# A written-out order of engine work: planner costs, a fourth output buffer, and a later values' product

## The chip, the cores and the metric

The kernel runs on one core of a Trainium2 chip. The metric is the device time of one execution in microseconds (us). Engines in the rows: PE is TensorE's matmul, PEld its weight load, DVE is VectorE, ACT is ScalarE, POOL is GpSimd, and SP is SyncE, which in this kernel issues nearly all transfers (SPq in the rows is its queue).

## The reference, cut to what matters

Three layers follow each other: windowed attention (B = 4 batches, 8 heads, S = 576 tokens, width 64), a gated layer with a spatial product over the tokens, and, last, four experts that are themselves causal attentions. The change touches only the experts' layer:

```python
logits = x @ w_gate                      # top 2 of E = 4 experts, softmax over them -> w
for e in range(E):
    q, k, v = x @ wq[e], x @ wk[e], x @ wv[e]
    scores = scale * (q @ k.transpose(0, 2, 1))
    scores = np.where(causal, -1e9, scores)
    a = softmax(scores)                  # over all 576 keys, causal
    ye = a @ v @ wo[e]
    out += (w of expert e, 0 if not chosen) * ye
```

The layer before it hands over one 512-wide row for each token; the product with its output weights is folded into wq, wk and wv.

## The kernel before, in words

All matmuls are 32-bit: a factor is split into a high part (a rounded copy, on ACT) and a low part (source minus high part, a subtraction), and three passes of products are added up (PASSES). PE's order is the order in which the Python code calls the matmuls. For the first two layers the order of the other engines is a list of names or is left to the compiler's scheduler. For the experts' layer a planner, class Flow, writes the order of ACT, DVE, POOL and SP while the PE code is generated: it keeps a clock `pe` of what PE has been given, and chains of items `(engine, ns, operation, after, ok)`. An item is put into its engine's order when, by the planned costs, the item before it in its chain is done (its `ns`, then `after`) and the engine is free. On the chip each engine runs its own order strictly, and semaphores hold an instruction until its operands and buffers are there; a planned cost is never a wait on the chip, it only sets places in the orders.

The experts' layer goes through 20 tiles, one for each batch b and block j of rows (j = 0 to 3 are 128 rows with 128, 256, 384 and 512 keys, j = 4 is the last 64 rows with all 576). For step s of the loop:

- `scores_b(*tiles[s])` (matmuls of L1084, and L1088 for j = 4) writes scores into two PSUM buffers (psS). Then, by the planner: row minima on DVE (L1114 or L1119), exponentials on ACT (L1115, L1124), the sums' inverses times the gates on DVE (L1136 to L1138), the scaling of the rows on POOL (`scale_rows`, L309), a transpose within blocks of 32 on DVE (L1162), four sends on SP to DRAM (`mid<-pB`, L1164), and one read back on SP (`read_back`, `pTB<-mid`, L1181; two for j = 4). The trip over DRAM completes the transposition. The buffers of the weights before (p) and after the trip (pT) are three each.
- `close_tile(tiles[s - LAG])`, LAG = 4, is the values' product of the tile four steps back: 16 to 40 matmuls L1234 that read pTB, then its copy `o` on ACT (L1247) and low part on DVE; and the tile's output product joins the list of work `todo`.
- five calls of `pull` take pieces from `todo`: the projections of the next batch (`proj`, `pq` L1022 and `pvB` L992) and the output products (`out_tile`, `pout`, six matmuls L1276), each followed by a copy to `ot` on ACT (L1281) and a store on SP (L1283, L1285). `ot` has 3 buffers, `o` has 11 (OBUFS) for each part.

In the last steps three tiles (y, a, z in the code: rows 2, 1, 0 of the last batch) are transposed on PE instead (`turn_b`, `ptB`, L1206, copied by L1212); `turn_b(y)` stands in step 18, the last of the loop, and the scores of z behind it.

`load_g(b)` brings the input of batch b in four chunks of 288 KB (`gf<-g_dram`, L887): for each chunk a high part on ACT (`x<-gf`, L894), a low part on POOL (`lo_part`, L274), and at the end the same for a tail (`both`, L903). Batch 0's is written before the planner starts, batch 1's is its first chain, and those of batches 2 and 3 run beside the steps.

Of the kernel before, what the change touches and what calls it, by code (L numbers as in the profile page):

```python
# [10 lines left out]
F32 = mybir.dt.float32  # L11
# [11 lines left out]
B, H, S, D = 4, 8, 576, 64  # L23
P = 128
DM = 512
# [7 lines left out]
FLT_MAX = 3.0e38  # L33
TOK = [(t * 128, min(128, S - t * 128)) for t in range(5)]
COL = [64, 192, 320, 448, 0]
OBUFS = 11
PASSES = ((0, 0), (0, 1), (1, 0))
ORDER = ((0, 1, 2, 3, 4), (4, 0, 1, 2, 3))
OPENING = """
# [202 lines left out]
def item(engine, ns, op, after=0.0, ok=None):  # L242
    return engine, ns, op, after, ok
# [3 lines left out]
def block_kernel(ctx, tc, qP, kP, v, w_in, wspT, bsp, w_outT, wcat, wo, relt, tri, out):  # L247
    nc = tc.nc
# [24 lines left out]
    def lo_part(lo, src, hi, engine=nc.vector):  # L273
        engine.tensor_sub(lo, src, hi.bitcast(F32))  # L274
# [56 lines left out]
    back, over, first, both = (t[:, :P] for t in u)  # L331
# [548 lines left out]
    both = []  # L880

    def load_g(b, pool):
        G = x if b % 2 == 0 else x2
        f = pool.tile([P, 4, S], F32, tag="gf", name=f"gf{b}", bufs=1)

        def fetch(k, after=0.0):
            return "SP", 400.0, lambda: nc.sync.dma_start(f[:, k, :], g_dram[b, k]), after, None  # L887

        def parts():
            first = 2 if b > 1 else 4  # L890
            for k in range(first):
                yield fetch(k, 6000.0 if k == first - 1 else 0.0)
            for k in range(4):
                yield "ACT", 626.0, lambda k=k: nc.scalar.copy(G[0][:, k, :S], f[:, k, :]), 0.0, None  # L894
                yield "POOL", 900.0, lambda k=k: lo_part(G[1][:, k, :S], f[:, k, :], G[0][:, k, :S], nc.gpsimd), 3000.0 if b > 1 and 0 < k < 3 else 0.0, None
                if k + first < 4:
                    yield fetch(k + first)
            c = slice(64 * (b % 2), 64 * (b % 2) + 64)

            def high():  # L900
                if b % 2 == 0:
                    both[:] = [gfp.tile([P, 4, P], F32R, tag=f"both{i}", name=f"both{b}_{i}") for i in range(2)]
                nc.scalar.copy(both[0][:, :, c], f[:, :, 0:64])  # L903

            yield "ACT", 400.0, high, 0.0, lambda: tails_done[0] >= b // 2
            yield "POOL", 500.0, lambda: lo_part(both[1][:, :, c], f[:, :, 0:64], both[0][:, :, c], nc.gpsimd), 0.0, None

        return G, list(parts())

# [11 lines left out]
    wk = ctx.enter_context(tc.tile_pool(name="wk", bufs=2, reuse_waits="tile"))  # L921
    wos = [wk.tile([P, 2, DM], F32R, name=f"wo{i}", bufs=1) for i in range(2)]
    for k in range(2):
        st = wk.tile([P, DM], F32, tag="ot", name=f"st_wo{k}", bufs=3)
        nc.sync.dma_start(st, wo[k * P : (k + 1) * P, :])
        split(wos[0][:, k, :], wos[1][:, k, :], st)
    x2 = [wk.tile([P, 4, S], F32R, name=f"x2{i}", bufs=1) for i in range(2)]
# [5 lines left out]
    flow = Flow()  # L933
# [8 lines left out]
    def leave(n, *items, delay=250.0):  # L942
        banks[n] = flow.add(items, rank=0, delay=delay)
        return banks[n]
# [206 lines left out]
    def cross_items(b, j):  # L1151

        p = sb_[b, j][0]
        e = 4 if j < 4 else 2
        n, w = (4 * (j + 1), 128) if j < 4 else (18, 64)
        mid = dram.tile([16 if j < 4 else 18, 32, 4, w], F32, tag=f"mid{w}", name=f"mid{b}_{j}", bufs=3)
        me = state[b, j]
        items = []
        cuts = [0, n * w] if n < 12 else [0, n * w // 2, n * w]
        for c0, c1 in zip(cuts, cuts[1:]):  # L1160
            flat = p[:, c0:c1]
            items.append(item("DVE", 130.0 + 1.12 * (c1 - c0), lambda flat=flat: nc.vector.transpose(flat, flat)))  # L1162
        def send(q):
            nc.sync.dma_start(mid[:n, :, q, :].rearrange("k i w -> i k w"), p[32 * q : 32 * q + 32, : n * w].rearrange("i (k w) -> i k w", w=w))  # L1164
            me["written"] = q == 3

        items += [item("SP", 500.0, lambda q=q: send(q), 0.0 if q < 3 else 5000.0) for q in range(4)]
        items.append(item("SP", 400.0, lambda: read_back(b, j, mid), 5000.0, lambda: tiles.index((b, j)) < 3 or tiles[tiles.index((b, j)) - 3] in closed))
        items.append(item("PE", 0.0, lambda: me.update(read=True)))
        return items  # L1170

# [2 lines left out]
    def read_back(b, j, mid):  # L1174
        e = 4 if j < 4 else 2
        n, w = (4 * (j + 1), 128) if j < 4 else (18, 64)
        cs = (n + 3) // 4
        pT = wk.tile([P, 16 * P], F32, tag="pT", name=f"pTB{b}_{j}", bufs=3)
        for c0, m, rows in ((0, n // 4, 128),) if j < 4 else ((0, 4, 128), (4, 1, 64)):
            src = mid[4 * c0 : 4 * c0 + rows // 32 * m].rearrange("(c k) i a w -> (k i) c (a w)", c=m)  # L1180
            nc.sync.dma_start(pT[:rows, c0 * 4 * w : (c0 + m) * 4 * w].rearrange("i (c w) -> i c w", c=m), src)  # L1181
        full = pT[:, : cs * 4 * w].rearrange("p (c a e q) -> p c a e q", a=4, e=e, q=32)

        def rhs(pr, c, o):
            kb = 64 if c == 4 else 128
            return full[:, c, :, 2 * pr + o, :] if j < 4 else full[:kb, c, 2 * o : 2 * o + 2, pr, :]

        sb_[b, j] = rhs
# [60 lines left out]
        flow.work(400.0 + (2 * (j + 1) * 212.0 if j < 4 else 2 * 9 * 120.0))  # L1249

    taken = {}
    stored = deque()

    def out_tile(b, t):
        flow.finish(taken[b, t])
        t0, tn = TOK[t][0], P
        o2 = OT.pop((b, t))
        if (b, t) == tiles[-1]:
            ot = wk.tile([P, DM], F32, tag="ot", name=f"ot{b}_{t}", bufs=3)
            for h, copy in enumerate((nc.vector.tensor_copy, nc.scalar.copy)):  # L1260
                c = slice(256 * h, 256 * h + 256)
                at, po = bank(f"pout{b}_{t}_{h}")
                n = 0
                for i, j in PASSES:
                    for pr in range(2):
                        nc.tensor.matmul(po[:, :256], o2[i][:, pr, :], wos[j][:, pr, c], start=(n == 0), stop=(n == 5))
                        n += 1
                leave(at, item(("DVE", "ACT")[h], 400.0, lambda copy=copy, c=c, po=po: copy(ot[:, c], po[:, :256])),
                      item(("SP", "ACT")[h], 400.0, lambda h=h, c=c: (nc.sync, nc.scalar)[h].dma_start(out[b, t0 : t0 + tn, c], ot[:, c])))
                yield 6 * 120.0  # L1270
            return
        at, po = bank(f"pout{b}_{t}")
        n = 0
        for i, j in PASSES:
            for pr in range(2):
                nc.tensor.matmul(po[:tn], o2[i][:, pr, :tn], wos[j][:, pr, :], start=(n == 0), stop=(n == 5))  # L1276
                n += 1
            if n < 6:
                yield 2 * 231.0
        ot = wk.tile([P, DM], F32, tag="ot", name=f"ot{b}_{t}", bufs=3)  # L1280
        items = [item("ACT", 580.0, lambda: nc.scalar.copy(ot[:tn], po[:tn]))]  # L1281
        if t < 4:
            items.append(item("SP", 400.0, lambda: nc.sync.dma_start(out[b, t0 : t0 + tn, :], ot)))  # L1283
        else:
            items += [item("SP", 500.0, lambda i=i: nc.sync.dma_start(out[b - 1 + i, t0:S, :], ot[64 * i : 64 * i + 64])) for i in range(2)]  # L1285
        stored.append(leave(at, *items))
        if len(stored) > 2:
            flow.finish(stored.popleft())
        yield 2 * 231.0


# [31 lines left out]
    def close_tile(t):  # L1323
        at, px = attend_b(*t)
        take_b(*t, at, px)
        b1, j1 = t
        if j1 < 4 or b1 % 2:
            todo.append(out_tile(b1, j1))
# [5 lines left out]
    for s in range(len(tiles) - 1):  # L1334
        b, j = tiles[s]
        if s % 5 == 0:
            if p_next is not None:
                through(p_next)
            if b + 1 < B:
                flow.finish(ahead)  # L1340
                p_next = proj(b + 1, G)
                todo.appendleft(p_next)
            if b + 2 < B:
                G, ahead = load(b + 2)
        if s >= 1:
            ready(tiles[s - 1])
        if s >= 3:
            flow.until(lambda: state[tiles[s - 3]]["written"])
        scores_b(*tiles[s])
        if s >= LAG:  # L1350
            close_tile(tiles[s - LAG])
        for i in range(5):
            pull((5500.0 if s < 1 else RATE if s < 15 else 4600.0 if s < 18 else 2000.0) / 5)
            if tiles[s] == a and i == 1:
                turn_b(*y)
            if tiles[s] == a and i == 3:
                ready(a)
                for chain in state[y]["home"]:
                    flow.finish(chain)
                flow.until(lambda: state[tiles[s - 2]]["written"])  # L1360
                scores_b(*z)
# [83 lines left out]
```

## Time and profile before

| | us |
|---|---|
| median of 3 runs (lowest, highest) | 464.69 (464.23, 466.42) |
| the profiled execution, its own time | 463.66 |
| its span, first to last instruction | 461.9 |
| PE busy in the span | 438.9 (95%) |
| DVE, ACT, POOL busy | 299.1, 252.5, 128.6 |
| mean granted TensorE clock | 0.987 of full speed |

The span is what the rows show; 1.8 us lie around it in that execution. The experts' layer begins at 278.5 us of the span with its first projection; the first scores come at 297.0, and the last instruction ends at 461.9. In rows of a timeline a group of like instructions is one line: its start, its length in us, engine, line of the kernel, operation, and in brackets how long the engine stood idle before it and what released it.

### The profile page before, as it was taken

To read this page: it belongs to the slowest core of one execution; us is meant where nothing else is said; L and a number is where in the kernel's file an instruction comes from. 1 tells how busy PE (TensorE), PEld (TensorE's weight loads), DVE (VectorE), ACT (ScalarE), POOL (GpSimd) and SP (SyncE) were. 2 spreads that over 40 slices of the span, in tenths; PEclk is the share of its full clock that TensorE was granted. 3 is DMA by queue.
4 is the path that set the end of the run, shared out by engine and by line. 5 is a ranking of instruction groups with operands and counts; after the bars stand their busy time and mean duration, and the time that the engine had idled before them with its cause. 6 is when DMAs were issued, how large, how long until landed. Compare 5 with 4: busy or idle time off the path is not lost.

```text
span 461.9 us, 11248 instructions
## 1 busy us (share of the span) xinstructions
PE 438.9 (95%) x4159; PEld 391.1 (85%) x4159; DVE 299.1 (65%) x1054; ACT 252.5 (55%) x774; POOL 128.6 (28%) x253
## 2 busy tenths in 40 slices
PE   7889999999999999999999999999969899999696
PEld 6568897898988999889989999998959898887474
DVE  6999999958786756773371223267776686776241
ACT  6987887746665344773253024467545454565441
POOL 2072312111022310204105002546765353341100
PEclk9999999999999999999999999999999999999889
DMA  8980565161513330004191600125877687598863
GB/s 259 336 306 19 189 217 163 38 201 69 165 37 105 103 114 28 1 1 142 33 340 68 220 4 2 53 72 111 249 205 203 186 203 200 144 208 255 189 216 92
DMA packets 56780, 66.37 MB, mean 144 GB/s; under 512 B 13715, under 2 KB 35859, under 8 KB 56341
## 3 DMA queue, kind: packets, MB, share of 16 engines
q1 hardware_dynamic: 56580, 65.51, 47.2%
q8 instruction: 33, 0.54, 0.5%
q14 instruction: 23, 0.18, 0.1%
q10 hardware_dynamic: 144, 0.13, 0.1%
HBM read 42.82 MB, written 22.81 MB: 142 GB/s over the span
## 4 chain that ended last, share of the span: by engine, by line
PE 69%; DVE 9%; DMA 7%; ACT 6%; SPq 3%; POOL 2%; issue 2%; ACTq 0%; DVEq 0%; POOLq 0%
PE pg L716 10%; PE pv L638 10%; PE pq L1022 9%; PE pu L701 8%; PE px L612 6%; PE pxB L1234 5%; PE pw L862 4%; PE pout L1276 3%; PE pt L584 3%; DVE pB L1162 3%; PE psB L1084 3%; SPq L1164 2%; DMA mid<-pB 2%; PE pg L719 2%; POOL pB L309 2%
## 5 line engine op out<-in xcount | busy, mean ns | idle before, releaser
L593 POOL TENSOR_SCALAR_AFFINE_SELECT pU<-pT 128x512 f32<-128x512 f32 (+1 forms) x32 | 21.4, 678 | 161.3 <-ACT pT L586 161.1
L297 ACT ACTIVATE p<-p,st 128x128 f32<-128x128 f32 x144 | 56.7, 396 | 13.3 <-DVE st L296 12.9
L716 PE MATMUL pg<-wsp,vn 128*128 128x288 f32 x384 | 58.7, 297 | 0.0
L701 PE MATMUL pu<-x,win 128*128 128x288 f32 x384 | 56.0, 298 | 0.8 <-ACT u L704 0.6
L638 PE MATMUL pv<-win,x 128*128 128x512 f32 x216 | 55.1, 399 | 0.0
L716 PEld LDWEIGHTS pg<-wsp,vn 128*128 128x128 f32 x384 | 53.2, 188 | 1.1 <-issue 0.5
L701 PEld LDWEIGHTS pu<-x,win 128*128 128x128 f32 x384 | 52.2, 188 | 2.1 <-ACT u L704 0.8
L1022 PE MATMUL pq<-x,W 128*128 128x288 f32 x384 | 53.9, 297 | 0.0
L1022 PEld LDWEIGHTS pq<-x,W 128*128 128x128 f32 x384 | 51.2, 188 | 1.6 <-issue 1.3
L638 PEld LDWEIGHTS pv<-win,x 128*128 128x128 f32 x216 | 39.1, 188 | 7.9 <-issue 0.5
L309 POOL TENSOR_SCALAR pB<-pB,stB 128x384 f32<-128x384 f32 (+4 forms) x64 | 35.8, 574 | 35.2 <-DVE stB L1138 13.8
L1115 ACT ACTIVATE pB<-pB,stB 128x128 f32<-128x128 f32 (+3 forms) x64 | 35.8, 560 | 13.9 <-DVE stB L1114 13.3
L586 ACT COPY pT<-pt 128x512 f32<-128x512 f32 (+1 forms) x40 | 21.6, 539 | 34.1 <-PE pt L584 34.0
L296 DVE CUSTOM_DVE_ANT_0 p<-ps,relm 128x128 f32<-128x128 f32 x128 | 31.3, 284 | 5.6 <-PE ps L538 2.6
L1162 DVE STREAM_TRANSPOSE pB<-pB 128x1024 f32<-128x1024 f32 (+3 forms) x28 | 27.1, 985 | 9.3 <-POOL pB L309 9.2
L1234 PE MATMUL pxB<-pTB,vt 128*64 128x128 f32 (+2 forms) x480 | 30.2, 273 | 2.4 <-DMA pTB<-mid 2.4
L724 DVE TENSOR_TENSOR g<-u,pg 128x288 f32<-128x288 f32 x32 | 14.1, 450 | 27.3 <-PE pg L719 27.1
L1234 PEld LDWEIGHTS pxB<-pTB,vt 128*64 128x64 f32 (+1 forms) x480 | 24.8, 143 | 7.3 <-issue 5.1
L1114 DVE CUSTOM_DVE_ANT_0 pB<-psB,trit 128x128 f32<-128x128 f32 (+3 forms) x64 | 28.6, 482 | 1.6 <-DMA mid<-pB 1.4
L1276 PE MATMUL pout<-wo,o 128*128 128x512 f32 x102 | 27.3, 412 | 0.8 <-ACT o L1247 0.8
L297 ACT ACTIVATION_READ_ACCUMULATOR p<-p,st 128x1 f32 x144 | 27.4, 190 | 0.0
L571 DVE TENSOR_TENSOR p<-p,st 128x512 f32<-128x512 f32 (+1 forms) x40 | 26.4, 662 | 0.5
(178 smaller groups left out, 908.7 us busy)
## 6 DMA issues: line engine op xcount, KB each, us to landing
q<-in_qP SPq DMA_DIRECT2D x20, 256.0 KB, 4.2
g_dram<-g SPq DMA_DIRECT2D x16, 288.0 KB, 2.8
gf<-g_dram SPq DMA_DIRECT2D x16, 288.0 KB, 4.8
raw<-in_w_in SPq DMA_DIRECT2D x8, 512.0 KB, 6.2
v<-in_v SPq DMA_DIRECT2D x16, 256.0 KB, 6.0
mid<-pB SPq DMA_DIRECT2D x16, 256.0 KB, 5.1
pTB<-mid SPq DMA_DIRECT2D x4, 1024.0 KB, 7.0
out<-ot SPq DMA_DIRECT2D x15, 256.0 KB, 4.8
```

The costliest lines, as they stand in the source:

```text
L296: lambda: nc.vector.tensor_tensor_reduce(s_view, ps_view, tab, -0.125, FLT_MAX, ALU.add, ALU.min, nm),
L297: lambda: nc.scalar.activation(s_view, s_view, AF.Exp, bias=nm, scale=-1.0, accum_out=sm),
L309: nc.gpsimd.tensor_scalar(p, p, r, 0.0, op0=ALU.mult, op1=ALU.add)
L638: nc.tensor.matmul(pv, x[i][:, k, t0 : t0 + P], win[j][:, k, 512:1024], start=(n == 0 and k == 0), stop=(n == 2 and k == 3))
L701: nc.tensor.matmul(pu[:, :HALF], win[i][:, k, m * P : (m + 1) * P], x[j][:, k, c], start=(n == 0 and k == 0), stop=(n == 2 and k == 3))
L716: nc.tensor.matmul(pg[:, :HALF], vn[i][k][:, m * P : (m + 1) * P], wsp[j][:, k, c], start=(n == 0 and k == 0), stop=False)
L1022: nc.tensor.matmul(pq[:, :HALF], W[i][c0 // CUT][:, k, c0 % CUT : c0 % CUT + P], G[j][:, k, c], start=(n == 0), stop=(n == 11))
L1114: item("DVE", 230.0 + 1.03 * kn, lambda: V.tensor_tensor_reduce(part(p, i), cut(two[pr][:, o, :kn]), cut(trit[:, 512 - q0 : 512 - q0 + kn] ...
L1115: item("ACT", 480.0 + 0.84 * kn, lambda: nc.scalar.activation(part(p, i), part(p, i), AF.Exp, bias=nm, scale=-1.0, accum_out=sm)),
L1162: items.append(item("DVE", 130.0 + 1.12 * (c1 - c0), lambda flat=flat: nc.vector.transpose(flat, flat)))
L1234: nc.tensor.matmul(px[64 * o : 64 * o + 64, pr, :qn], vt[:kb, c, (2 * pr + o) * 64 : (2 * pr + o) * 64 + 64], rhs(pr, c, o), start=(c == 0 ...
L1276: nc.tensor.matmul(po[:tn], o2[i][:, pr, :tn], wos[j][:, pr, :], start=(n == 0), stop=(n == 5))
```

## The change

It has six parts: (1) planned costs of `load_g`'s items, and the low parts of batches 0 and 1 go to DVE; (2) the same for the tail's low part; (3) planned times after the last send and after the read back, by block; (4) `ot` gets a fourth buffer, `o` one fewer; (5) the planner waits for the fourth store back in place of the third, and plans a copy into `ot` no earlier than 4.5 us behind that store; (6) `close_tile` comes behind one or two pulls if by the plan the weights are not back. The diff shows one of the three places where `ot` is taken.

```diff
-OBUFS = 11
+OBUFS = 10
...
             for k in range(4):
-                yield "ACT", 626.0, lambda k=k: nc.scalar.copy(G[0][:, k, :S], f[:, k, :]), 0.0, None
-                yield "POOL", 900.0, lambda k=k: lo_part(G[1][:, k, :S], f[:, k, :], G[0][:, k, :S], nc.gpsimd), 3000.0 if b > 1 and 0 < k < 3 else 0.0, None
+                yield "ACT", 670.0, lambda k=k: nc.scalar.copy(G[0][:, k, :S], f[:, k, :]), 0.0, None
+                on, ns, engine = ("DVE", 850.0, nc.vector) if b < 2 else ("POOL", 1430.0, nc.gpsimd)
+                yield on, ns, lambda k=k, engine=engine: lo_part(G[1][:, k, :S], f[:, k, :], G[0][:, k, :S], engine), 2000.0 if b > 1 and 0 < k < 3 else 0.0, None
...
-            yield "POOL", 500.0, lambda: lo_part(both[1][:, :, c], f[:, :, 0:64], both[0][:, :, c], nc.gpsimd), 0.0, None
+            yield "POOL", 740.0, lambda: lo_part(both[1][:, :, c], f[:, :, 0:64], both[0][:, :, c], nc.gpsimd), 0.0, None
...
-            ot = wk.tile([P, DM], F32, tag="ot", name=f"ot{b}_{t}", bufs=3)
+            ot = wk.tile([P, DM], F32, tag="ot", name=f"ot{b}_{t}", bufs=4)
...
-        items += [item("SP", 500.0, lambda q=q: send(q), 0.0 if q < 3 else 5000.0) for q in range(4)]
-        items.append(item("SP", 400.0, lambda: read_back(b, j, mid), 5000.0, lambda: tiles.index((b, j)) < 3 or tiles[tiles.index((b, j)) - 3] in closed))
+        items += [item("SP", 500.0, lambda q=q: send(q), 0.0 if q < 3 else (1900.0, 3500.0, 3500.0, 5100.0, 6200.0)[j]) for q in range(4)]
+        items.append(item("SP", 400.0, lambda: read_back(b, j, mid), (3600.0, 4600.0, 5400.0, 7000.0, 4600.0)[j], lambda: tiles.index((b, j)) < 3 or tiles[tiles.index((b, j)) - 3] in closed))
...
-    stored = deque()
+    stored = []
...
-        stored.append(leave(at, *items))
-        if len(stored) > 2:
-            flow.finish(stored.popleft())
+        wait = 250.0
+        if len(stored) > 3:
+            flow.finish(stored[-4])
+            wait = max(wait, stored[-4][2] + 4500.0 - flow.pe)
+        stored.append(leave(at, *items, delay=wait))
...
         scores_b(*tiles[s])
-        if s >= LAG:
-            close_tile(tiles[s - LAG])
+        due = tiles[s - LAG] if s >= LAG else None
         for i in range(5):
+            if due and (state[due]["read"] or i == 2):
+                close_tile(due)
+                due = None
             pull((5500.0 if s < 1 else RATE if s < 15 else 4600.0 if s < 18 else 2000.0) / 5)
```

## Rows read from the trace of the kernel before

**Rows 1.** Windows of the experts' stage: length, busy time of each engine, PEclk, DMA share, GB/s.

```profile
280.00:290.00 10.00, 10.00 (x78) 10.00 (x77) 3.95 (x8) 5.37 (x12) 4.56 (x7) 1.00 0.01 2
...
340.00:350.00 10.00, 5.83 (x53) 5.08 (x52) 6.27 (x18) 4.16 (x14) 4.60 (x10) 0.83 0.97 241
...
420.00:430.00 10.00, 10.00 (x109) 8.15 (x108) 3.78 (x11) 3.88 (x10) 0.76 (x2) 1.00 0.74 204
430.00:440.00 10.00, 6.36 (x43) 4.59 (x43) 4.50 (x21) 5.46 (x16) 2.27 (x4) 0.83 0.85 190
```

**Rows 2.** Timeline of PE around its first long gap, and the same product later.

```profile
342.07 0.79 PE L1084 MATMUL psB<-k,q 64*128 64x384 f32 x6 [1.73 <-DVE stB L1114]
345.30 3.25 PE L1234 MATMUL pxB<-pTB,vt 128*64 128x128 f32 x32 [2.44 <-DMA pTB<-mid]
...
381.51 1.97 PE L1234 MATMUL pxB<-pTB,vt 128*64 128x128 f32 x32
```

**Rows 3.** Timeline of PE near the end of the loop.

```profile
429.42 1.19 PE L1276 MATMUL pout<-wo,o 128*128 128x512 f32 x4
432.66 2.72 PE L1206 MATMUL ptB<-ident,pB 128*128 128x128 f32 x12 [2.05 <-POOL pB L309]
435.03 1.94 PE L1276 MATMUL pout<-wo,o 128*128 128x512 f32 x4
438.55 0.89 PE L1084 MATMUL psB<-k,q 64*128 64x128 f32 x12 [1.58 <-ACT pTB L1212]
...
446.74 0.66 PE L1206 MATMUL ptB<-ident,pB 128*128 128x128 f32 x4
```

**Rows 4.** Timeline of ACT in the same stretch.

```profile
421.36 0.58 ACT L1281 COPY ot<-pout 128x512 f32<-128x512 f32 x1 [3.64 <-DMA out<-ot]
...
430.07 0.59 ACT L1281 COPY ot<-pout 128x512 f32<-128x512 f32 x1 [3.01 <-DMA out<-ot]
...
436.45 0.58 ACT L1281 COPY ot<-pout 128x512 f32<-128x512 f32 x1 [1.80 <-DMA out<-ot]
```

**Rows 5.** Timelines of DVE and POOL in the same stretch.

```profile
431.29 0.17 DVE L1136 TENSOR_SCALAR stB<-stB 128x4 f32<-128x4 f32 x1 [5.81 <-ACT pB L1115]
...
432.55 0.42 DVE L1114 CUSTOM_DVE_ANT_0 pB<-psB,trit 128x256 f32<-128x256 f32 x1 [0.68 <-DMA mid<-pB]
...
432.02 2.27 POOL L309 TENSOR_SCALAR pB<-pB,stB 128x384 f32<-128x384 f32 x4 [11.26 <-DMA mid<-pB]
```

**Rows 6.** Timeline of SP's queue: issues, not transfers.

```profile
374.50 0.38 SPq L1181 DMA_DIRECT2D pTB<-mid  x1
...
422.76 0.53 SPq L1283 DMA_DIRECT2D out<-ot  x1
...
425.87 6.73 SPq L1164 DMA_DIRECT2D mid<-pB  x6
```

**Rows 7.** DMA issues from 255 us on: count, KB each, median us from issue to landing.

```profile
mid<-pB SPq DMA_DIRECT2D x16, 256.0 KB, 5.1
pTB<-mid SPq DMA_DIRECT2D x4, 1024.0 KB, 7.0
out<-ot SPq DMA_DIRECT2D x15, 256.0 KB, 4.8
```

**Rows 8.** POOL's low parts of the batch inputs: duration min/median/max in ns.

```profile
L274 POOL TENSOR_TENSOR x<-gf,x x16: 1406/1430/1446, 247.2 to 356.2; 128x576 fp32r<-128x576 f32 x16
```

**Rows 9.** Timelines of DVE and POOL: low parts, and one small DVE instruction twice.

```profile
236.16 0.96 DVE L274 TENSOR_TENSOR wc<-st_wc,wc 128x772 fp32r<-128x772 f32 x1 [0.50 <-ACT wc L277]
...
336.92 1.43 POOL L274 TENSOR_TENSOR x<-gf,x 128x576 fp32r<-128x576 f32 x1 [2.33 <-ACT x L894]
...
344.16 0.16 DVE L1138 TENSOR_TENSOR stB<-stB,gt 128x4 f32<-128x4 f32 x1
...
337.06 1.31 DVE L1138 TENSOR_TENSOR stB<-stB,gt 128x4 f32<-128x4 f32 x1
```

**Rows 10.** Waits of SP's queue from 255 us on: us in total, times, longest.

```profile
SPq L1181 <- DMA mid<-pB: 28.9, 16, 3.8
```

More of the change, by code (lines that the diff above doesn't have):

```diff
@@ L923, in block_kernel @@
     for k in range(2):
-        st = wk.tile([P, DM], F32, tag="ot", name=f"st_wo{k}", bufs=3)
+        st = wk.tile([P, DM], F32, tag="ot", name=f"st_wo{k}", bufs=4)
         nc.sync.dma_start(st, wo[k * P : (k + 1) * P, :])
@@ L1279, in out_tile @@
                 yield 2 * 231.0
-        ot = wk.tile([P, DM], F32, tag="ot", name=f"ot{b}_{t}", bufs=3)
+        ot = wk.tile([P, DM], F32, tag="ot", name=f"ot{b}_{t}", bufs=4)
         items = [item("ACT", 580.0, lambda: nc.scalar.copy(ot[:tn], po[:tn]))]
```

## Prediction

> **What bounds the kernel now.** The page's head comes first: PE is busy for 438.9 of 461.9 us, and all the matmuls stay. So the change can win only what PE loses by waiting in the experts' stage and what a lower clock after a wait costs. The windows show where that is: from 340 to 350 us PE is busy for 5.83 of 10 us, from 430 to 440 for 6.36, each time with the granted clock at 0.83, while the ten microseconds ahead of the latter are full [rows 1]. A mean of 0.83 between the two levels (2.4 and 1.2 GHz) is a third of the window at the lower one.
>
> The timeline of PE then says what it waited for. *First gap:* the second half of step 7's scores waits 1.73 us for DVE's row minima, then the values' product of tile (0, 3) waits 2.44 us for its weights from DRAM, and its 32 matmuls take 3.25 us where the same 32 take 1.97 us later [rows 2]. *Second gap:* the transposes of y wait 2.05 us for POOL's scaling, the scores of z 1.58 us for ACT's copy of those transposes. At the lower clock four output matmuls take 1.94 us, where four take 1.19 us just before, and the twelve transposes 2.72 us, where four take 0.66 [rows 3].
>
> The third view is ACT's timeline in the second gap. Three times a copy into `ot` stands at the head of ACT's order and waits for a store to free its buffer: 3.64, 3.01 and 1.80 us [rows 4]. The second one, up to 430.07, stands ahead of the last exponential of y. DVE's sums follow at 431.29 after 5.81 us idle, POOL's scaling at 432.02, PE's transposes at 432.66 [rows 3 to 5]: one chain. The third, up to 436.45, stands ahead of the copies for which z waits. The first costs PE nothing that shows: its ten microseconds are full [rows 1].
>
> **The change part by part.**
>
> *Fourth buffer, and copies planned 4.5 us behind the fourth store back.* A copy now waits for the store four copies back. The copy at 430.07 came to the head of ACT at 427.06 and would wait for the store issued at 422.76 [rows 4, 6]; with the median 4.8 us of a store [rows 7] that is free at 427.6: 0.5 us in place of 3.01. The third waits for a store that had landed by 430.0, since the copy before it waited for that one: nothing. So y's chain moves ahead by 2.5 us, and the 2.05 us go. For z's 1.58 us there are two ends. The row minima of the tile between, a, begin at 432.55 after a wait for sends that had to leave their buffer [rows 5], and some of those sends stood in SP's queue from 425.87 on for 6.73 us [rows 6]. If those stay late, only the third wait goes: 1.8 us is the low end of the whole tail. If they come earlier because no store stalls ahead of them, both waits go, 3.63 us, with the low clock's 0.75 (1.94 - 1.19) and 0.74 (2.72 - 3 x 0.66): 5.1 us, the high end. I take the 3.63 us less the 0.5 us left, and half of the 1.49 us of clock: **3.9 us**.
>
> *Values' product later if its weights are not back.* It moves behind two pulls of 780 ns, by whole pieces three pieces of four projection matmuls, planned at 532 ns each: 1.6 us. They would run within the 2.44 us wait [rows 2], so it shrinks to 0.84 us. If the clock holds then, another 3.25 - 1.97 = 1.28 us come back: 2.9 us is the high end. The low end is nothing: the planner decides by its own clock, and if by its costs tile (0, 3) is back in time, the order stays. Those costs now say 5.1 + 7.0 us for a tile of this size where they said 10, so it is likelier to come out late than before. I take **1.6 us**. The 1.73 us ahead of it stay. What is late next: tile (1, 3) read its weights from 374.50 on, and with the median 7.0 us they landed at 381.50, its product begins at 381.51 [rows 2, 6, 7]. There is no slack there: PE's pace cannot fall below this trip, which is why I count one gap and no more.
>
> *Planned times of the trips.* No instruction changes, only places in SP's queue. Where the plan has a read back sooner (5.5 us in place of 10 for j = 0), SP may stand before it longer. It stood there 16 times for 28.9 us already, 3.8 us at the longest [rows 10]. Below: nothing, the sends behind are not ready; above: 3.8 us on a trip that PE waits for. I take nothing here and make the upper end a rival.
>
> *Eight low parts from POOL to DVE.* POOL's took 1.43 us each [rows 8]. For DVE the nearest row is 772 wide, 0.96 us, so 576 wide are about 0.72 us [rows 9]: 2.9 us for each of two batches. Between 280 and 290 us, where three of batch 1's run, PE is full with DVE busy for 3.95 of 10 us [rows 1], so the other 6 us hide them; batch 0's likewise stand behind the spatial product. Without that cover a product's PSUM would come free 0.72 us later, below the 1.6 us of a group of projections: nothing, at most 0.72 us in all.
>
> DVE's multiply of four numbers takes 0.16 us at 344.16, but 1.31 us at 337.06, and then ends with a POOL low part that began 0.14 us before it [rows 9]. The Trainium skill (SBUF — State Buffer, section "SBUF: two separate sides") says that a DVE instruction with two SBUF inputs and a GpSimd instruction that reads SBUF exclude each other, the later one standing still; this trace agrees. By it the moved low parts would hold up POOL's instructions by up to 0.72 us each and spare DVE waits of up to 1.43 us, and the sum would change only if PE waited for one of these, which the full window denies.
>
> *Planned costs of POOL (900 to 1430, 500 to 740), the shorter pause (3000 to 2000), 10 `o` buffers.* The whole chain for an input is planned 0.5 us longer; the costs meet the measured 1.43 us [rows 8]. Ten `o` buffers hold while fewer than ten output products are open. Nothing each; a wait for an `o` would stop ACT and then PE, at least the 0.4 us of a copy.
>
> The sum is 3.9 + 1.6 = 5.5 us: span 456.4, the profiled execution 458.2. The median lies 1.03 us above the profiled one, so the median becomes **459.2 us**.
>
> **Rivals.**
>
> *A. The tail's low end alone.* The plan thinks the weights back, and the sends before a stay late: 1.8 us, 462.9. For it: the plan's clock is near the edge for tile (0, 3), and the 6.73 us on SP's queue. Against: part of that queue's delay came from the stores themselves.
>
> *B. The change doesn't do what it says.* The transfers set the pace near the end: the fourth buffer fills as the third did, since DMA drains no faster, and ACT waits as before: 464.7. For it: DMA is busy for 0.97 of the first gap and 0.85 of the second [rows 1]. Against: in the window with the 3.01 us wait it is 0.74.
>
> *C. Slower.* Read backs issued sooner hold SP in front of sends. Place: the trips of the tiles with j = 3 of the first three batches, which have no slack. Price: 3.8 us each [rows 10], less the 1.6 us of the later product: 2.2 us, three times 6.6; with 1.28 us of low clock at two places that had none, 9.2. Against the tail's 3.9 us that leaves 5.3 us, 470.0. It decides against the change from about 2.9 us a trip on ((3.9 + 3 x 1.6) / 3). Against it: for j = 3 and 4 the plan issues the read back later than before (5.1 and 6.2 us after the last send, where it had 5).
>
> *D. Everything.* 2.9 and 5.1 us, and the 1.73 us of DVE [rows 2]: 9.7 us, 455.0. It needs step 7's DVE rows to come sooner, for which only the truer POOL costs speak.
>
> **How the numbers follow.** About 0.5% (2.3 us) is what a measurement here can tell from no change. Chances: forecast (456.5 to 462.3) 0.52; A 0.14; B 0.12; C 0.10; D 0.12. Of A a third may fall beyond 2.3 us. Faster 0.52 + 0.12 + 0.05 = 0.69, same 0.09 + 0.12 = 0.21, slower 0.10. The range takes in D and B and leaves out C and the ends: 454.8 to 465.0; the forecast's own is 456.5 to 462.3.
>
> **What would show it.** ACT's waits for stores fall from 8.45 us (3.64 + 3.01 + 1.80 [rows 4]) to under 1.5; the transposes of y start without POOL as releaser; the scores of z start 3 to 5 us sooner against the scores of a. In step 7 projection matmuls stand between the scores and the 32 values' matmuls, whose wait is under 1 us, at full clock. The low parts of batches 0 and 1 stand on DVE at about 0.7 us. I am wrong if ACT still waits for stores, if the order of step 7 is the old one, or if new waits of PE for pTB appear at tiles with j = 3.

## The result and the profile after

| | before | after |
|---|---|---|
| median, timed beside each other (14 runs each) | 466.13 us (464.11 to 471.41) | 461.62 us (460.45 to 463.93) |
| the profiled execution, its own time | 463.66 us | 461.94 us |
| its span | 461.9 us | 460.2 us |

The ratio is 0.9912, with a 95% interval of 0.9889 to 0.9934: 0.88% faster, where 1.18% was forecast (459.2 of 464.69). An execution can fall into a slower state, and the ratio is worked out without such runs, here without the one at 471.41 us, so it is not the quotient of the medians (0.9903). A second timing, in the third group of runs below, gave 0.9921 (0.9891 to 0.9951). The profiled execution of before was faster than all 14 of its runs here, so the two traces differ by 1.7 us where the ratio stands for about 4. Readings below are therefore held against several executions where there are several.

**First gap.** Windows of after (columns as in [rows 1]), then PE's timeline in the first gap, which answers to [rows 2].

```profile
280.00:290.00 10.00, 10.00 (x78) 10.00 (x77) 6.22 (x11) 5.56 (x13) 0.96 (x4) 1.00 0.01 2
340.00:350.00 10.00, 7.86 (x76) 6.95 (x78) 6.77 (x23) 6.46 (x21) 5.39 (x11) 1.00 0.75 227
...
430.00:440.00 10.00, 6.86 (x50) 5.52 (x48) 4.21 (x19) 4.10 (x12) 0.21 (x1) 0.71 0.89 212
```

```profile
340.40 0.80 PE L1085 MATMUL psB<-k,q 64*128 64x384 f32 x6 [0.85 <-DVE stB L1115]
341.13 1.84 PE L1023 MATMUL pq<-x,W 128*128 128x288 f32 x12
344.71 1.97 PE L1235 MATMUL pxB<-pTB,vt 128*64 128x128 f32 x32 [1.74 <-DMA pTB<-mid]
...
352.17 0.95 PE L1235 MATMUL pxB<-pTB,vt 128*64 128x64 f32 x20 [1.58 <-DMA pTB<-mid]
```

The reader is to see three things. Twelve projection matmuls now stand ahead of the values' product of (0, 3); the product runs at full clock (1.97 us, was 3.25); and the wait is not gone but shorter, 1.74 us, with a new one of 1.58 us behind it, for the weights of (0, 4). In a second profiled execution of the change the product waits 2.67 us and takes 2.49, and (0, 4) waits for nothing. From 280 to 290 us DVE takes the low parts (6.22 us busy, was 3.95), and PE stays full.

**Second gap.** PE's timeline (it answers to [rows 3]), and all of ACT's waiting for a store in this trace ([rows 4] had 8.45 us).

```profile
429.57 1.04 PE L1207 MATMUL ptB<-ident,pB 128*128 128x128 f32 x8
433.68 0.66 PE L1207 MATMUL ptB<-ident,pB 128*128 128x128 f32 x4 [3.08 <-DVE stB L1115]
...
436.04 1.54 PE L1085 MATMUL psB<-k,q 64*128 64x128 f32 x12
437.51 2.83 PE L1235 MATMUL pxB<-pTB,vt 128*64 128x128 f32 x24
```

```profile
436.67 0.59 ACT L1282 COPY ot<-pout 128x512 f32<-128x512 f32 x1 [0.68 <-DMA out<-ot]
```

ACT waits 0.68 us for one store, and POOL no longer holds up y's transposes. But four of the twelve now wait 3.08 us for DVE: they need a PSUM buffer in which the scores of a still lie. The chain of waits says why these are late.

```profile
412.22 7.83 DMA mid<-pB
...
427.39 4.40 DMA mid<-pB
...
431.96 0.43 DVE pB L1115
```

The last send of (2, 4) takes 7.83 us to land. The read back of (2, 4) (L1182) stands at the head of SP's queue until then, and behind it wait a store and the sends of (3, 3), whose data were ready at 416.55 (the end of their last transpose on DVE). SP's timeline:

```profile
420.20 1.56 SPq L1182 DMA_DIRECT2D pTB<-mid  x2
421.87 0.53 SPq L1284 DMA_DIRECT2D out<-ot  x1
422.50 0.36 SPq L1165 DMA_DIRECT2D mid<-pB  x1
...
423.57 8.80 SPq L1165 DMA_DIRECT2D mid<-pB  x7
```

These eight sends are four of (3, 3) and, behind them, four of (3, 4). The last send of (3, 3) lands 4.40 us after 427.39, its p buffer comes free, and only then does DVE begin the row minima of a (431.96, after 4.17 us idle). Before, the same buffer was waited for 0.68 us behind ACT [rows 5].

**Where the time went, by stretches.** Starts of scores in PE's timelines cut each profiled execution: those of (1, 0) (326.22 us in after), of (2, 0) (364.65), of y (416.69), and the span's end.

| profiled execution | to (1, 0) | to (2, 0) | to y | to the end |
|---|---|---|---|---|
| before | 327.01 | 40.67 | 51.14 | 43.1 |
| after, two executions | 326.22, 326.22 | 38.43, 38.80 | 52.04, 52.10 | 43.5, 42.6 |
| after without the buffer, two | 326.44, 327.00 | 39.10, 39.26 | 52.02, 52.03 | 42.9, 43.7 |
| buffer alone | 327.15 | 41.22 | 51.15 | 44.2 |
| product later alone | 328.21 | 38.73 | 51.15 | 44.4 |
| splits alone | 326.66 | 38.83 | 52.26 | 44.4 |
| times of trips alone | 327.48 | 40.75 | 51.99 | 43.9 |

What the change wins lies between 327 and 365 us: 1.4 to 2.2 us in its four executions with and without the buffer. Behind that it gives 0.9 us back (a product of 24 matmuls at 372.15 waits 0.78 us for a low part of k on DVE). Of the tail's forecast 3.9 us nothing stands in these traces: it is 43.5 and 42.6 us long, and was 43.1. Two executions of one kernel differ there by up to 0.9 us, so a smaller difference in the last column says nothing.

### The profile page after: what moved, and what is told of

The parts are those of the page before. It is cut to its first block, busy times and chain, and to the rows that moved or that the text cites. A ratio compares the mean times of both kernels' runs of the same rounds, so it can differ in the third digit from the quotient of the medians.

```text
span 460.2 us, 11249 instructions
## 1 busy us (share of the span) xinstructions
PE 436.4 (95%) x4159; PEld 389.0 (85%) x4159; DVE 303.6 (66%) x1062; ACT 251.2 (55%) x774; POOL 118.1 (26%) x245
## 4 chain that ended last, share of the span: by engine, by line
PE 62%; DVE 11%; DMA 9%; ACT 8%; SPq 4%; POOL 3%; issue 2%; POOLq 0%; ACTq 0%; DVEq 0%
PE pg L716 11%; PE pv L638 10%; PE pu L701 8%; PE pq L1023 7%; PE px L612 6%; DMA mid<-pB 5%; PE pw L862 4%; DVE pB L1163 3%; PE pt L584 3%; PE pxB L1235 3%; SPq L1165 2%; POOL pB L309 2%; ACT pB L1116 2%; PE pg L719 2%; PE psB L1085 2%
```

## The experiments

Ratios are to the kernel before, timed in the same group. "Resampled" marks a 95% interval of a difference of medians, got by drawing from the runs again and again. Three groups of kernels: 1 to 4 (before: 465.22 us, 35 runs); 5 and 7 to 9 (466.31, 24 runs); 5 once more, 6, 10 and 11 (465.55, 23 runs).

**1. The fourth buffer alone.**

```diff
-OBUFS = 11
+OBUFS = 10
-... tag="ot", ... bufs=3)
+... tag="ot", ... bufs=4)
```

> The kernel before with four buffers for ot and ten for o, and nothing else; the order of every engine stays as it was. Theory P (the prediction's): ACT's three waits for stores go but for about 0.5 us, the 2.05 us wait of y's transposes for POOL goes, and the time falls by 1.8 to 5.1 us. Rival R (read from the profile after): y's transposes come earlier but their second half waits for the PSUM buffer that a's scores hold, because a's row minima still begin only when the sends of tile (3, 3) have left their buffer; the gain is given back there and the time falls by 0 to 1 us.

Measured: 465.16 us, ratio 0.9995 (0.9973 to 1.0017). PE's and DVE's timelines:

```profile
435.83 0.66 PE L1206 MATMUL ptB<-ident,pB 128*128 128x128 f32 x4 [2.63 <-DVE stB L1114]
...
438.19 0.89 PE L1084 MATMUL psB<-k,q 64*128 64x128 f32 x12 [0.77 <-ACT pTB L1212]
...
444.95 3.63 PE L1234 MATMUL pxB<-pTB,vt 128*64 128x128 f32 x32 [2.00 <-DMA pTB<-mid]
```

```profile
434.12 0.42 DVE L1114 CUSTOM_DVE_ANT_0 pB<-psB,trit 128x256 f32<-128x256 f32 x1 [3.71 <-DMA mid<-pB]
```

ACT's copies wait for no store here. The 2.05 and 1.58 us of [rows 3] became 2.63 for a's row minima, 0.77 for ACT, and 2.00 for the read back of (3, 3): 5.40 where there were 3.63. Behind the wait that was removed stood others. The planner's delay of copies, the other half of the forecast's first part, changes no place in any engine's order, with or without the rest; so this kernel is the whole of that part. The theory of the prediction (1.8 to 5.1 us) is refuted, and the rival that stands beside it (0 to 1 us) holds.

**2. One product later.** Step 7's product behind two pulls, nothing else.

```diff
-        if s >= LAG:
-            close_tile(tiles[s - LAG])
         for i in range(5):
+            if s >= LAG and i == (2 if s == 7 else 0):
+                close_tile(tiles[s - LAG])
```

> The kernel before with one values' product moved: that of tile (0, 3) comes behind the first two pulls of step 7 (twelve projection matmuls), as in the kernel after; all planned costs and buffers stay. Theory P: the 2.44 us wait for its weights shrinks by about 1.7 us, its 32 matmuls run at full clock (1.97 us in place of 3.25), and the time falls by 1.6 to 2.9 us. Rival R: the next product, of tile (0, 4), then waits for its own weights by nearly as much (1.58 us in the kernel after), and the time falls by less than 1 us.

Measured: 463.42 us, 0.9958 (0.9933 to 0.9983), that is 1.9 us (0.8 to 3.1). PE's timeline in both gaps:

```profile
343.79 1.86 PE L1022 MATMUL pq<-x,W 128*128 128x288 f32 x12
346.31 1.97 PE L1234 MATMUL pxB<-pTB,vt 128*64 128x128 f32 x32 [0.66 <-DMA pTB<-mid]
...
433.23 2.74 PE L1206 MATMUL ptB<-ident,pB 128*128 128x128 f32 x12 [2.61 <-POOL pB L309]
...
439.07 0.89 PE L1084 MATMUL psB<-k,q 64*128 64x128 f32 x12 [1.67 <-ACT pTB L1212]
```

The step of the prediction holds by itself: 1.86 us of work inside the wait, full clock behind it. The next product, of (0, 4), waits 0.46 us in this trace, so the rival's condition came in a small size. This is the only product that the change moves. By the orders that the planner writes, the new condition moves none with the old planned costs, none with the trips' times, and none with the costs of the splits; it takes both.

**3. The splits alone** (parts 1 and 2 of the change, all their lines).

```diff
-... "POOL", 900.0, ... nc.gpsimd), 3000.0 ...
+on, ns, engine = ("DVE", 850.0, nc.vector) if b < 2 else ("POOL", 1430.0, nc.gpsimd)
```

> The kernel before with the new engine and planned costs for the splits of the batch inputs alone (low parts of batches 0 and 1 on DVE; 670, 850, 1430, 740 and the pause of 2000 ns). PE's order stays. Theory P: 0, at most 0.72 us to either side. Rival R: the order of SP and POOL that follows from these costs carries the gain seen before step 7 and at step 10 (0.44 and 1.19 us waits of scores for DVE are gone in the kernel after): 1 to 2.5 us faster.

Measured: 464.32 us, 0.9983 (0.9962 to 1.0004). PE's timeline:

```profile
336.69 2.48 PE L1235 MATMUL pxB<-pTB,vt 128*64 128x128 f32 x24 [3.31 <-DVE stB L1138]
...
345.64 1.97 PE L1235 MATMUL pxB<-pTB,vt 128*64 128x128 f32 x32 [0.16 <-PE psB L1085]
...
365.49 0.89 PE L1085 MATMUL psB<-k,q 64*128 64x128 f32 x12
...
372.96 1.53 PE L1235 MATMUL pxB<-pTB,vt 128*64 128x128 f32 x24 [0.76 <-DVE k L274]
```

and, from the kernel before, the scores of (2, 0):

```profile
367.68 0.89 PE L1084 MATMUL psB<-k,q 64*128 64x128 f32 x12 [1.19 <-DVE stB L1119]
```

In the stretch up to (2, 0) the splits win as much as the later product does (38.83 and 38.73 us, was 40.67); together the two win no more (38.4 to 39.3). Part of it is the 1.19 us wait of the scores of (2, 0), which is gone with the splits and stays without them (1.21 us in experiment 2). Another part seems to be the same wait that the later product works on: a delay ahead of the product of (0, 3), here 3.31 us at (0, 2), hides the trip. Which of the items on ACT, DVE, POOL and SP that change places does this is not shown. Behind it the splits cost 1.1 us again (52.26, was 51.14), so the rival's waits went as it said, but the time by 0.8 us (from 1.8 won to 0.2 lost) where it had 1 to 2.5.

**4. The times of the trips alone** (part 3).

```diff
-0.0 if q < 3 else 5000.0
+0.0 if q < 3 else (1900.0, 3500.0, 3500.0, 5100.0, 6200.0)[j]
-read_back(b, j, mid), 5000.0,
+read_back(b, j, mid), (3600.0, 4600.0, 5400.0, 7000.0, 4600.0)[j],
```

> The kernel before with the planned times of the trips over DRAM alone; PE's, DVE's and POOL's orders stay, some read backs change places with sends in SP's queue, among them two of the tiles with j = 0 that now stand ahead of the read back of j = 4. Theory P: 0. Rival R: up to 1 us faster, from the scores of step 10. The rival C of the prediction: slower by 2 us or more, with new waits of PE for pTB at tiles with j = 3.

Measured: 464.79 us, 1.0001 (0.9974 to 1.0028): nothing, as forecast. Places in SP's queue and some of ACT's change, and the first gap stays: the product of (0, 3) still waits 2.23 us. Small new waits for weights appear, 0.25 us at (1, 3), where rival C of the prediction looked for one, and 0.44 us at (1, 4); at its size of 2.2 us a trip it is refuted.

**5 and 6. The change without its buffer,** twice, and the change itself again.

```diff
-OBUFS = 10
+OBUFS = 11
-... tag="ot", ... bufs=4)
+... tag="ot", ... bufs=3)
...
-        stored.append(leave(at, *items, delay=wait))
+        stored.append(leave(at, *items))
+        if len(stored) > 2:
+            flow.finish(stored.popleft())
```

> The kernel after with three buffers for ot, eleven for o and the old rule for stores: splits, trips and the later product alone. The orders of all engines are those of the kernel after. Theory S (the fourth buffer is worth nothing as long as the sends of tile (3, 3) stand behind the read back of tile (2, 4) in SP's queue): about as fast as the kernel after, 0.8 to 1% faster than before. Theory P (the prediction's, in what is left of it): the fourth buffer still carries about 2 us of the gain, so only 0.3 to 0.5% faster than before.

> The kernel after with three buffers for ot, once more beside it. Theory S (the fourth buffer is worth nothing while the sends of (3, 3) are held): within 1 us of the kernel after. Theory P: 2 us slower than the kernel after.

> The kernel after once more, beside the three others of this set on the same chip: 0.66 to 1.1% faster than before, as measured first.

Measured without the buffer: 463.93 us, 0.9949 (0.9922 to 0.9975), and in the third group 463.36 us, 0.9956 (0.9930 to 0.9983); beside the latter the change gave 461.31 us. The medians of that group differ by 2.05 us (resampled, 0.1 to 3.1), those of both groups of after and both without the buffer by 2.35 us (0.8 to 3.1), though the latter were not all timed beside each other. Theory S, by which the buffer is worth nothing here, is not borne out; the 0.5% and 0.4% without it are what theory P said. So here the buffer pays, though alone it does not: between 1.3 us gained and 0.8 lost. Some 1 us would fit both. The traces don't say where: without the buffer ACT's copies wait again,

```profile
ACT ot L1282 <- DMA out<-ot: 9.0, 5, 4.8
```

(list of ACT's waits: us in total, times, longest), and yet the table's last column shows the same tail. This stays open.

**7 and 8. The read back of (2, 4) behind the sends of (3, 3) in SP's queue,** in the changed kernel with and without the buffer.

```diff
-0.0 if q < 3 else (1900.0, 3500.0, 3500.0, 5100.0, 6200.0)[j]
+0.0 if q < 3 else 9000.0 if (b, j) == (2, 4) else (1900.0, 3500.0, 3500.0, 5100.0, 6200.0)[j]
```

> The kernel after with one thing changed: the planned time after the last send of tile (2, 4) is 9000 ns in place of 6200, which puts its read back behind the sends of tile (3, 3) in SP's queue; the other engines' orders stay. Theory S: the sends of (3, 3) leave about 3 to 4 us sooner, a's row minima no longer wait for them, the 3.08 us wait of y's second transposes shrinks below 1 us, and the time falls by 2 to 4 us against the kernel after (about 1.4 to 1.7% against before). Rival D (the transfers themselves set the pace there): the sends land at the same time, and the time stays as in the kernel after. A third way: the read back of (2, 4) now lands too late, its product at step 18 waits, and nothing is won.

> The read back of tile (2, 4) behind the sends of (3, 3), as in the run before, with three buffers for ot. Theory S: once the sends are not held, ACT's waits for stores are what y and z wait for, so it loses 2 us or more against the run with four buffers. Rival D: the same time as with four buffers.

Measured: 460.42 us, 0.9881 (0.9852 to 0.9909, 6 runs), and without the buffer 462.04 us, 0.9891 (0.9852 to 0.9929, 7 runs). SP's and PE's timelines of the first:

```profile
417.86 3.02 SPq L1165 DMA_DIRECT2D mid<-pB  x2
...
422.26 2.00 SPq L1165 DMA_DIRECT2D mid<-pB  x2
```

```profile
430.88 2.35 PE L1235 MATMUL pxB<-pTB,vt 128*64 128x64 f32 x40 [2.78 <-DMA pTB<-mid]
...
435.02 1.60 PE L1207 MATMUL ptB<-ident,pB 128*128 128x128 f32 x12
```

DVE's timeline:

```profile
429.12 0.42 DVE L1115 CUSTOM_DVE_ANT_0 pB<-psB,trit 128x256 f32<-128x256 f32 x1
```

The four sends of (3, 3) go out from 417.86 on and are issued by 424.3 (the change: from 422.50 on, the last at 427.39). The row minima of a wait for none of them and begin at 429.12 (was 431.96), and the transposes of y wait for nothing, so the queue's order was behind the 3.08 us. The product of (2, 4), which stands ahead of these transposes, now waits 2.78 us for the read back that was put behind, so this trace alone could hide a wait of theirs; experiment 10 has them ahead of it. The tail is 41.4 us long in both profiled executions. The gain is less than theory S said (1.19% where it had 1.4 to 1.7%), since its third way came true as well. Between four and three buffers the medians differ by 1.6 us (resampled, -2.0 to 2.6), which does not tell S from D.

**9. Two products one place deeper,** to close what is left of the first gap (and all other products where the kernel before had them).

```diff
-            if due and (state[due]["read"] or i == 2):
+            if due and (i == {7: 3, 8: 3}.get(s, 0)):
```

> The kernel after with the values' products of tiles (0, 3) and (0, 4) behind three pulls in steps 7 and 8 by hand (after: two and none); all others at once. If the waits of 1.74 and 1.58 us at these two products are lost time, they shrink by about 0.5 and 1.6 us and the time falls by 1 to 2 us against the kernel after. Rival: PE's pace there is set by the trips, the time only moves to the waits behind (scores of steps 9 to 11 for DVE), and the time stays within 0.5 us of the kernel after.

Measured: 463.3 us, 0.9947 (0.9921 to 0.9973), no better than the change: the 1 to 2 us did not come. PE's timeline:

```profile
345.84 2.83 PE L1235 MATMUL pxB<-pTB,vt 128*64 128x128 f32 x32 [3.09 <-DMA pTB<-mid]
...
367.31 0.89 PE L1085 MATMUL psB<-k,q 64*128 64x128 f32 x12 [1.85 <-DVE stB L1120]
```

The product of (0, 3) begins between 344.5 and 346.4 us in all kernels of this study, before among them, and in nine of the fourteen traces the profile names its weights as what it waited for. So it seems that its weights set that time, and a later place only changes what PE does until then.

**10. Read back behind, and its product later too.** Kernel 7, and in step 18 the product of (2, 4) behind two pulls, so behind y's transposes.

```diff
-            if due and (state[due]["read"] or i == 2):
+            if due and (i == 2 or (state[due]["read"] and s < 18)):
```

> The kernel after with the read back of tile (2, 4) behind the sends of (3, 3) (planned 9000 ns) and its product in step 18 behind the transposes of y. With the read back alone moved, the sends left sooner and y's transposes waited for nothing, but the product of (2, 4) itself waited 2.78 us. If these 2.78 us are lost time, they shrink to under 1 us and the time falls by 2 to 3 us against the kernel after, to 1.3 to 1.6% faster than before. Rival D (the transfers near the end set the pace): the wait moves on to the products of (3, 3) or of y, and the time is that of the kernel after.

Measured: 459.68 us (459.11 to 460.29, 5 runs), 0.9881 (0.9854 to 0.9907): 1.63 us below the change in the same group (resampled, 0.9 to 3.5). That is less than the 2 to 3 us expected, and its ratio is that of experiment 7, so what the later product adds to the moved read back is not told apart. PE's timeline and a step of the chain of waits:

```profile
429.25 2.23 PE L1207 MATMUL ptB<-ident,pB 128*128 128x128 f32 x12 [0.63 <-POOL pB L309]
431.41 1.82 PE L1235 MATMUL pxB<-pTB,vt 128*64 128x64 f32 x40
...
440.29 1.97 PE L1235 MATMUL pxB<-pTB,vt 128*64 128x128 f32 x32 [1.24 <-DMA pTB<-mid]
```

```profile
431.68 8.47 DMA pTB<-mid
```

The transposes of y, now ahead of the product of (2, 4), wait 0.63 us, and that product waits for nothing. The tail is 39.4 us. A part of the wait has moved on, as rival D had it: the product of (3, 3) waits 1.24 us for its read back, which takes 8.47 us.

**11. Small stores.** Each store of rows 0 to 511 writes 64 of its 512 columns, 32 KB in place of 256; seven eighths of those outputs are left unwritten. The orders are those of the change.

```diff
-nc.sync.dma_start(out[b, t0 : t0 + tn, :], ot)
+nc.sync.dma_start(out[b, t0 : t0 + tn, 0:64], ot[:, 0:64])
```

> The kernel after, whose stores of the blocks j = 0 to 3 write the first 64 of 512 columns alone (32 KB in place of 256), so that most of the output is left unwritten; every engine's order stays, the number of issues too. Rival D (the bytes of the stores set the pace near the end): the sends of (2, 4) and (3, 3) land sooner, the read back holds SP for less, the waits of 1.16 us at step 17 and 3.08 us at y's transposes go, and the time falls by 3 to 5 us. Theory S (the order in SP's queue alone): the read back still stands before the sends, and the time falls by less than 1 us.

Measured: 456.03 us (454.99 to 457.02, 5 runs), 0.9803 (0.9775 to 0.9831), 5.28 us below the change in the same group (resampled, 4.2 to 7.1). PE's timeline of the change in that group, all waits from 417 to 445 us, and below it that of the small stores, the same four places:

```profile
419.38 1.97 PE L1235 MATMUL pxB<-pTB,vt 128*64 128x128 f32 x32 [0.95 <-DMA pTB<-mid]
...
433.41 0.66 PE L1207 MATMUL ptB<-ident,pB 128*128 128x128 f32 x4 [2.60 <-DVE stB L1115]
...
435.77 0.89 PE L1085 MATMUL psB<-k,q 64*128 64x128 f32 x12 [0.79 <-ACT pTB L1213]
...
442.56 1.97 PE L1235 MATMUL pxB<-pTB,vt 128*64 128x128 f32 x32 [2.03 <-DMA pTB<-mid]
```

```profile
418.83 1.97 PE L1235 MATMUL pxB<-pTB,vt 128*64 128x128 f32 x32
...
429.22 1.47 PE L1207 MATMUL ptB<-ident,pB 128*128 128x128 f32 x12
...
432.34 0.89 PE L1085 MATMUL psB<-k,q 64*128 64x128 f32 x12 [0.70 <-ACT pTB L1213]
...
437.02 1.97 PE L1235 MATMUL pxB<-pTB,vt 128*64 128x128 f32 x32
```

The waits add up to 6.37 and 0.70 us, and the tails are 42.6 and 36.6 us long: 5.7 of the 6.0 us are these waits. The read back at the head of SP's queue goes at 417.27 in place of 420.42. The number of packets is the same (39,652 and 39,608 from 255 us on), so the tail waits for bytes, through the places in SP's queue. Rival D of this experiment holds, theory S does not. That the same load took away what the fourth buffer alone was to win fits this, but no run shows it.

## Why the prediction was right, and where it was not

**Right: direction and range.** 461.62 us lies inside 454.8 to 465.0 and inside the forecast's own 456.5 to 462.3; but the forecast ratio, 0.988, lies just outside the measured interval. That the sum of 5.5 us came close to the 4.1 to 4.5 us measured is in part luck, as its larger term did not come as it was worked out.

**Right by itself, in part in the change: the values' product later, 1.6 us.** Alone 1.9 us (0.8 to 3.1), by the mechanism of the prediction. Inside the change the sign that its wait would be under 1 us failed: it is 1.74 and 2.67 us in the two executions, and 2.75 and 3.34 without the buffer. The wait for DVE ahead of it had shrunk (0.85 and 0.35 us, was 1.73), and PE stood longer before the weights instead. In the first execution the three waits there, 0.85, 1.74 and 1.58 us, add up to the 4.17 us of before (1.73 + 2.44); the stretch is shorter by the clock (3.25 - 1.97 = 1.28 us) and by the 1.19 us of (2, 0), which the splits took away. That the splits win about as much in this stretch when alone was not foreseen.

**Nothing for splits, trips and the other planned costs: right in number.** -0.17% (-0.38 to +0.04) and +0.01% (-0.26 to +0.28). For the splits the reason was not: their trace wins 1.8 us up to (2, 0) and loses 1.1 us behind it, and the prediction had neither, so that they nearly cancel is luck. The moved low part takes the time that was worked out for it (0.72 us):

```profile
L274 DVE TENSOR_TENSOR x<-gf,x x8: 751/757/760, 247.0 to 290.6; 128x576 fp32r<-128x576 f32 x8
```

(durations in ns, least, median, longest). That these parts move no time by themselves does not make them idle: without them the planner leaves the product where it was.

**Wrong: the tail, 3.9 us.** The failed step is "*If they come earlier because no store stalls ahead of them, both waits go, 3.63 us*". Stores no longer stalled, ACT's waits fell from 8.45 to 0.68 us as said, and yet the sends ahead of a stayed late: what stalled ahead of them in SP's queue was a read back that waits for the sends before it, not a store. That is rival A's condition, but even its 1.8 us did not come with the buffer alone (between 1.3 us gained and 0.8 lost), since the row minima of a took over as the releaser of y's transposes, and the read back of (3, 3) behind them. The sign at z came in part: its scores start 10.18 and 9.70 us behind those of a (was 11.80; with the buffer alone 9.72; without it 11.69 and 11.31), so 1.6 to 2.1 us sooner where 3 to 5 were forecast. But from there to the end it takes longer, 24.16 and 23.93 us and with the buffer alone 25.51, where it took 23.35 before and 22.54 and 23.39 without the buffer. What the buffer won at z was given back behind it in these traces. In the timings of the change the buffer still gave 2.05 us (0.1 to 3.1), by a way that is not shown.

The term for the clock was mis-sized too: the prediction set twelve transposes at full clock at three times 0.66 us, but they take 1.47 us (experiment 11), so the 2.72 us of before cost 1.25 us and not 0.74.

**Rival B was half right.** Transfers do set the pace near the end (experiment 11), but PE feels them through SP's queue and the p buffers, not through ACT's copies. The copies' waits went and the time fell, so it did not come true. The 0.74 of DMA share in the window of the 3.01 us wait was a weak reason against it: from 425 to 435 us of that trace, while the sends that mattered were under way, the share is 0.94.

**A sign of being wrong came, but not by rival C's mechanism.** A new wait for the weights of (2, 3), a tile with j = 3, appears, 1.16 us in the change, 0.95 again. It is there with the buffer alone (0.93), the later product alone (0.67) and the splits alone (0.87) as well, where no planned time of a read back is changed. Nor is it that PE came sooner: with the buffer alone the scores of y start 0.7 us later than before, and the product behind them waits all the same. With the small stores it is gone, so the stores' bytes have a part in it; whether before has it in other executions than its one trace is not shown. Nor was the slack of (1, 3) nothing, as the prediction read from a median landing time: in the change its product starts 6.27 us behind the issue of its read back (7.01 before) and waits for nothing.

## What to carry to other kernels

When an instruction at the head of an engine's order waits, look up what the next releaser of the same buffer is and when it came: a wait removed is worth only the distance to that one, and experiment 1 shows that it can be nothing. In a queue that issues both, put sends ahead of a read back that must wait for its own sends, and give the product that needs the read back a later place (the two together won 1.63 us here). Where a planner writes the orders, compare the orders first: here one part moved nothing, and another moved its one product only beside the planned costs of two others.

## What the runs showed of the hardware

Landing times under load are far from the medians of a whole stage. Transfers of the change from 255 us on, then from 405 to 440 us alone (count, KB, median us from issue to landing):

```profile
pTB<-mid SPq DMA_DIRECT2D x4, 1024.0 KB, 6.5
...
pTB<-mid SPq DMA_DIRECT2D x7, 512.0 KB, 4.4
```

```profile
pTB<-mid SPq DMA_DIRECT2D x2, 1024.0 KB, 9.2
...
pTB<-mid SPq DMA_DIRECT2D x2, 512.0 KB, 9.1
```

The prediction worked with medians of the stage [rows 7]: 7.0 us for the large read back, where the two of the change's tail took 9.2. Stores of 32 KB took 3.8 us in the median from 255 us on, those of 256 KB 4.4: an eighth of the bytes lands only 0.6 us sooner. But with the small stores the read backs of the tail (405 to 440 us) landed in 6.4 and 6.5 us, where the change had 9.2 and 9.1. The Trainium skill (DMA: Bandwidth & Descriptors, section "Specifications") names 512 bytes as the least size for the full rate. From 255 us on 11,218 of the change's 39,608 packets are smaller, and at a DMA share of 0.98 the transfers reach 290 GB/s over ten microseconds (experiment 10, 415 to 425 us). No run here changes the size of packets and leaves the bytes as they are.

A wait of about the same length was followed by the lower clock in one execution and not in another: behind 2.61 us, in experiment 2, twelve transposes took 2.74 us at a granted clock of 0.56, while behind 2.63 us in experiment 1 four took 0.66 us at 1.00. Some 3 us after the change's wait of 3.08 us y's 24 matmuls took 2.83 us, at 0.50; in the second execution, after 2.60 us, 1.53 us, at 1.00. So the forecast's half of 1.49 us for clock could not have been settled from one trace.

The timings have the mean granted clock of single runs, and it goes with the time. Of 82 runs of before, 37 at a clock of 0.985 or less have a median of 466.7 us, 43 at 0.987 to 0.989 one of 464.4. The mean clock is 0.987 in these 82 runs, 0.991 in the 24 without the buffer and 0.994 in the 26 of the change. At equal clock the buffer is worth about half of its 2.35 us: 462.1 and 463.1 us at 0.993, 461.0 and 462.2 at 0.996 (medians of 3 to 10 runs). So a part of what the change wins comes with the clock; whether shorter waits keep the clock up or a better clock shortens the waits is not shown.
